# A fused attention and two gated MLPs on one core: MLP blocks of 512 tokens in phases of three ff chunks

## The chip, the cores and the metric

The kernel runs on one core of a Trainium2 chip. The metric is the device time of one execution in microseconds (us). An execution's record gives the span from its first to its last instruction, which is a little shorter than the device time.

## What is computed

Attention with a cumulative bias over 4 batches, 8 heads, 576 positions and head size 64 gives 2304 tokens of 512 features. Two MLPs follow, each with 1536 inner features (ff). The first gates by a sigmoid, the second multiplies two projections:

```python
def _moe_ref(x, w_gate, w_val, w_out):
    gate = 1.0 / (1.0 + np.exp(-(x @ w_gate)))
    val = x @ w_val
    return (gate * val @ w_out).astype(np.float32)

def _moe2_ref(x, w_a, w_b, w_out):
    a = x @ w_a
    b = x @ w_b
    return (a * b @ w_out).astype(np.float32)
```

The activations are float32 and the weights float64 in memory.

## The kernel before

**Attention** goes head by head and ends when all heads' outputs stand, transposed, in `x_sb` (128 partitions x 4 groups of features x 2304 tokens). `attention()` also prepares the first weight tiles on the side. It is emitted in an order by due times and is hardly touched by the change.

**The MLPs** (`mlps`) cut the 1536 inner features of each MLP into 12 chunks of 128, so 24 in all, and take them in phases: six phases of four chunks, three for each MLP. Within a phase all 2304 tokens pass in blocks of `NB` = 384, so a phase has six steps. One step does, for each of its chunks:

- *up* (line 689): one group of matmuls for the gate and one for the value. Every product is made in three passes of 32-bit "round" matmuls (lines 276 to 278), the high half of one operand with the high and the low half of the other, and the low half with the high one. With four groups of features a chunk has 2 x 4 x 3 = 24 matmuls of 128 x `NB`.
- *g* (ACT, line 698) brings the gate out of PSUM, *hf* (DVE, line 702) multiplies it with the value's PSUM bank, *hh* (POOL, line 713) rounds to the high half of h, *hl* (DVE, line 716) subtracts for the low half. h has six tiles, g and hf two each.

Then *dn* (line 727) multiplies the step's h with the output weights. In the first MLP its results stand with features on partitions (four pieces of 128 x `NB`); in the second, with tokens on partitions (one piece of 128 x 512 for each 128 tokens). *ye* adds a piece to what earlier phases left (DVE, line 751), or copies it in the first phase of an MLP (ACT, line 749). The down matmuls of a step must all be issued before the third chunk of the next step goes up (`behind`, line 693). At the start of a step, two halves of the block's input, `xs`, have been made by ACT (line 676) and DVE (line 679).

**Weights** arrive by SP's queue as float64 in three raw buffers of 512 KB each. ACT takes an absolute value (line 224), DVE does four integer and scaling steps (lines 225 to 232), ACT writes the high half (line 243), POOL the low half (line 244). The converted tiles stand in slots: five for the gate matrices, six for the value matrices, six for the output matrices (`NSL`); a tile goes to slot (chunk modulo slots) and is not loaded before the slot's last reader is done. Eight tiles (`early`) are converted wholly within attention; three more have all but their last two steps (lines 243 and 244) done there.

**The order** on each engine is fixed when the program is built. `Schedule.emit` plays the operations through with assumed durations and, on each engine, takes the ready one with the smallest due time. The engines then run in that order and wait by semaphores.

Of the kernel before, what the change touches and what calls it, by code (L numbers as in the profile page):

```python
# [119 lines left out]
def attn_mlp_kernel(  # L120
# [26 lines left out]
    SR = S // NR  # L147
    KD = DM // 128
    KF = DFF // 128
    NB = 384  # L150


    phases = [[0, 1, 2, 3], [4, 5, 6, 7], [8, 9, 10, 11], [12, 13, 14, 15], [16, 17, 18, 19], [20, 21, 22, 23]]
    scale = 1.0 / float(D) ** 0.5
    NEG = -1e9

# [13 lines left out]
    xs0 = const.tile([128, 2, KD, NB], F32R, name="xs0")  # L170


    NSL = [5, 6, 6]
    wt = {}
    early = [(i, m) for m in range(2) for i in range(3)] + [(3, 0), (3, 1)]

    def w_alloc(pool, which):
        for i, m in which:
# [14 lines left out]
    NRAW = 3  # L193
# [428 lines left out]
    def mlps():  # L622
        def tile1(shape, dtype, name):
            return alone(ctx, shape, dtype, name)

        NMX = NB
        h_t = [tile1([128, 2, NMX], F32R, f"h{i}") for i in range(6)]
        g_t = [tile1([128, NMX], FP32, f"g{i}") for i in range(2)]
        hf_t = [tile1([128, NMX], FP32, f"hf{i}") for i in range(2)]
        xs_t = [xs0, tile1([128, 2, KD, NMX], F32R, "xs1")]  # L630
# [12 lines left out]
            "u": [0],  # L643
        })
        op = sc.op
        NP1 = 3

        steps, first, last = [], [], []
        for p in range(len(phases)):
            n = NB  # L650
            first.append(len(steps))
            ts = list(range(0, NT, n))
            steps += [(p, t, n) for t in ts]
            last.append(len(steps) - 1)
        begin = [sum(0.055 * n for _, _, n in steps[:i]) for i in range(len(steps))]
        chain = [None]

        def step(i):
            p, t1, N = steps[i]
            ts = slice(t1, t1 + N)  # L660
            t0 = begin[i]
            MM = 0.00042 * N + 0.001
            cs = phases[p]


# [19 lines left out]
            for e, c in enumerate(cs):  # L685
                for m in range(2):
                    key = (i, c, m)

                    def mm(key=key, c=c, m=m):
                        xs = sc.get("xs", i)  # L690
                        run(passes(sc.get("ps", key)[:, 0:N], wk(c, m), [(xs[:, 0, k, 0:N], xs[:, 1, k, 0:N]) for k in range(KD)]))

                    behind = [("dn", i - 1, d) for d in range(KD)] if e == 2 else []
                    op(("up",) + key, "PE", 12 * MM, mm, xdeps + behind + [("wr", c, m), chain[0]], t0 + 4 * e + 2 * m,
                       acq=("ps", key), rel=("xs", i) if e == len(cs) - 1 and m == 1 else None)
                    chain[0] = ("up",) + key
                g, u = (i, c, 0), (i, c, 1)
                op(("g", i, c), "ACT", 0.06 + N * 0.00083, lambda c=c, g=g: nc.scalar.activation(  # L698
                    out=sc.get("g", (i, c))[:, 0:N], in_=sc.get("ps", g)[:, 0:N],
                    func=ACTF.Sigmoid if p < NP1 else ACTF.Copy), [("up",) + g], t0 + 4 * e + 1,  # L700
                    acq=("g", (i, c)), rel=("ps", g))
                op(("hf", i, c), "DVE", 0.07 + N * 0.00104, lambda c=c, u=u: nc.vector.tensor_tensor(  # L702
                    out=sc.get("hf", (i, c))[:, 0:N], in0=sc.get("ps", u)[:, 0:N], in1=sc.get("g", (i, c))[:, 0:N],
                    op=ALU.mult),
                    [("up",) + u, ("g", i, c)], t0 + 4 * e + 3, acq=("hf", (i, c)), rel=(("ps", u), ("g", (i, c))))
            for e, c in enumerate(phases[p]):
                t = t0 + 4 * e + 3

                def src(c=c):
                    return sc.get("hf", (i, c))[:, 0:N]  # L710

                before = [("hl", i - 1, c2) for c2 in phases[steps[i - 1][0]]] if i else []
                op(("hh", i, c), "Pool", 0.245 + N * 0.00083, lambda c=c, src=src: nc.gpsimd.tensor_scalar(  # L713
                    sc.get("h", (i, c))[:, 0, 0:N], src(), 1.0, 1.0, ALU.mult, ALU.mult),
                    [("hf", i, c)] + before, t, acq=("h", (i, c)))
                op(("hl", i, c), "DVE", 0.07 + N * 0.00104, lambda c=c, src=src: nc.vector.tensor_tensor(  # L716
                    out=sc.get("h", (i, c))[:, 1, 0:N], in0=src(), in1=f32(sc.get("h", (i, c))[:, 0, 0:N]), op=ALU.subtract),
                    [("hh", i, c)], t, rel=("hf", (i, c)))
# [5 lines left out]
            for d in range(pieces):  # L724
                key = (i, "d", d)

                def mm(d=d, key=key):
                    hs = [sc.get("h", (i, c)) for c in phases[p]]
                    ws = [wtile(c, 2) for c in phases[p]]
                    ps = sc.get("ps", key)  # L730
                    sl = slice(d * 128, (d + 1) * 128)
                    if p < NP1:
                        run(passes(ps[:, 0:N], [(w[:, 0, sl], w[:, 1, sl]) for w in ws], [(h[:, 0, 0:N], h[:, 1, 0:N]) for h in hs]))
                    else:
                        run(passes(ps, [(h[:, 0, sl], h[:, 1, sl]) for h in hs], [(w[:, 0], w[:, 1]) for w in ws]))

                n = N if p < NP1 else DM
                op(("dn", i, d), "PE", 3 * len(phases[p]) * MM * n / N, mm, hdeps + wdeps, t0 + 18 + d, acq=("ps", key),
                   rel=tuple(("h", (i, c)) for c in phases[p]) if d == pieces - 1 else None)
                if p < NP1:  # L740
                    dst = y_of[d][:, ts]
                else:
                    dst = acc_sb[:, t1 // 128 + d]
                start = p in (0, NP1)

                def evac(d=d, key=key, dst=dst, n=n, start=start):
                    ps = sc.get("ps", key)[:, 0:n]
                    if start:
                        nc.scalar.copy(out=dst, in_=ps)
                    else:  # L750
                        nc.vector.tensor_tensor(out=dst, in0=ps, in1=dst, op=ALU.add)

                deps = [("dn", i, d)]
                if p == NP1:
                    deps += [("xl", j2, 0) for j2 in range(first[NP1 - 1], first[NP1])]
                op(("ye", i, d), "ACT" if start else "DVE", 0.07 + n * (0.00083 if start else 0.00104), evac, deps,
                   t0 + 18.5 + d, rel=("ps", key))
                if p == len(phases) - 1:
                    r = t1 // 128 + d
                    op(("od", r), "SP", 0.5, lambda r=r, dst=dst: nc.sync.dma_start(  # L760
                        out=out[r * 128:(r + 1) * 128, :], in_=dst), [("ye", i, d)], t0 + 19 + d)

        for i in range(len(steps)):
            step(i)
# [1 line left out]
        for n, m in order:  # L766
# [3 lines left out]
            if o in phase_of:  # L770
                i = last[phase_of[o]]
                deps = [("dn", i, d) for d in range(KD)] if m == 2 else [("up", i, o, m)]
            weights(sc, n, m, deps, begin[first[phase_of[n]]] - 24 + 4 * (n % 4) + (16 if m == 2 else 0), part=1 if (n, m) in order[len(early):len(early) + NRAW] else None)
        sc.emit()

    with tc.manual_schedule():
# [47 lines left out]
```

## Time and profile before

| | |
|---|---|
| time, median of 3 (lowest to highest) | 1149.31 us (1147.91 to 1152.03) |
| profiled execution: its own time, its span | 1150.44 us, 1148.7 us |
| PE busy | 1107.2 us, 6152 matmuls |
| PE weight loads busy | 1039.6 us |
| DVE, ACT, POOL busy | 631.2, 357.7, 299.9 us |
| mean granted TensorE clock | 0.998 |

The busy share of an engine counts its overlapped instructions once. A matmul's own duration in the trace includes its run through the array, which the next matmul overlaps; what a stream of matmuls costs is read from the distance of their starts. A wait printed behind an instruction is the idle time of its engine just before it and the instruction that ended it.

### The profile page before, as it was taken

Reading aid. Unit: us, or ns where it says so; the run is one execution under the profiler, and the core shown is the slowest. Engines: PE = TensorE matmul, PEld = TensorE weight load, DVE = VectorE, ACT = ScalarE, POOL = GpSimd, SP = SyncE. Lnnn points to the kernel's source line nnn. Section 1 sums busy time; section 2 is a strip of 40 time slices with the busy share of each in tenths; the row PEclk is TensorE's granted clock in tenths of the full one; section 3 lists DMA queues with packets and bytes.
Section 4 is the critical chain, followed back from the end, with each engine's and each line's share of the span. In section 5 each row is a group of like instructions: output and inputs, shape, how many; then the busy total and the mean of one; then the engine's idle time right before and its main releaser. Section 6 shows DMA issues by size and latency. Waiting matters only on the chain.

```text
span 1148.7 us, 16112 instructions
## 1 busy us (share of the span) xinstructions
PE 1107.2 (96%) x6152; PEld 1039.6 (91%) x6152; DVE 631.2 (55%) x1015; ACT 357.7 (31%) x635; POOL 299.9 (26%) x364
## 2 busy tenths in 40 slices
PE   2999999999999999999999999999999999999998
PEld 1787777798999999999999999899999999999997
DVE  5788788728223783337943369522487334653322
ACT  2575666534122431112311133322343111322100
POOL 2245555554001340002410024200233101311100
PEclk9999999999999999999999999999999999999999
DMA  3566676533000230002310013200122000200001
GB/s 110 149 180 159 172 171 161 135 92 111 1 1 18 79 109 16 1 1 74 102 46 1 1 43 105 74 1 1 37 92 92 1 1 3 71 28 29 29 28 55
DMA packets 69743, 74.08 MB, mean 64 GB/s; under 512 B 28551, under 2 KB 53311, under 8 KB 69666
## 3 DMA queue, kind: packets, MB, share of 16 engines
q1 hardware_dynamic: 66514, 68.08, 20.7%
q10 hardware_dynamic: 2896, 4.81, 1.7%
q8 instruction: 49, 0.80, 0.3%
q14 instruction: 28, 0.23, 0.1%
q0 software_dynamic: 256, 0.15, 0.1%
HBM read 57.65 MB, written 5.60 MB: 55 GB/s over the span
## 4 chain that ended last, share of the span: by engine, by line
PE 78%; DVE 8%; DMA 5%; POOL 3%; issue 3%; ACT 2%; SPq 0%; ACTq 0%; POOLq 0%; DVEq 0%
PE ps L277 22%; PE ps L278 22%; PE ps L276 22%; PE ps_x L570 5%; PE ps_g L498 2%; DVE u L227 2%; POOL w L244 1%; DVE raw L229 1%; DVE h L716 1%; DVE hf L702 1%; DVE raw L232 1%; PE ps_e L535 1%; PE ps_e L536 1%; DVE u L225 1%; PE ps_g L503 1%
## 5 line engine op out<-in xcount | busy, mean ns | idle before, releaser
L276 PE MATMUL ps<-xs,w 128*128 128x384 f32 x1152 | 385.0, 334 | 0.0
L278 PE MATMUL ps<-xs,w 128*128 128x384 f32 x1152 | 385.0, 334 | 0.0
L277 PE MATMUL ps<-xs,w 128*128 128x384 f32 x1152 | 384.9, 334 | 0.0
L713 POOL TENSOR_SCALAR h<-hf 128x384 fp32r<-128x384 f32 x144 | 91.9, 638 | 576.8 <-DVE hf L702 576.8
L702 DVE TENSOR_TENSOR hf<-ps,g 128x384 f32<-128x384 f32 x144 | 79.9, 555 | 281.7 <-PE ps L278 280.9
L276 PEld LDWEIGHTS ps<-xs,w 128*128 128x128 f32 x1152 | 216.3, 188 | 0.7
L277 PEld LDWEIGHTS ps<-xs,w 128*128 128x128 f32 x1152 | 216.3, 188 | 0.7
L278 PEld LDWEIGHTS ps<-xs,w 128*128 128x128 f32 x1152 | 216.3, 188 | 0.0
L698 ACT ACTIVATE g<-ps 128x384 f32<-128x384 f32 x144 | 70.8, 491 | 435.4 <-PE ps L278 435.3
L244 POOL TENSOR_TENSOR w<-raw,w 128x512 fp32r<-128x512 f32 x72 | 101.0, 1403 | 131.9 <-ACT w L243 129.2
L716 DVE TENSOR_TENSOR h<-hf,h 128x384 fp32r<-128x384 f32 x144 | 88.9, 618 | 83.1 <-POOL h L713 83.1
L276 PE MATMUL ps<-h,w 128*128 128x384 f32 x288 | 97.3, 338 | 2.2 <-POOL h L713 2.0
L278 PE MATMUL ps<-h,w 128*128 128x384 f32 x288 | 97.0, 337 | 2.1 <-POOL w L244 2.1
L570 PE MATMUL ps_x<-pt,vx 128*128 128x320 f32 (+4 forms) x448 | 95.6, 365 | 2.3 <-DMA vx<-in_vm_dram 1.1
L277 PE MATMUL ps<-h,w 128*128 128x384 f32 x288 | 97.0, 337 | 0.6 <-DVE h L716 0.6
L511 DVE TENSOR_REDUCE nm<-ps_g 128x1 f32<-128x512 f32 (+4 forms) x160 | 77.0, 531 | 37.1 <-PE ps_g L503 37.0
L570 PEld LDWEIGHTS ps_x<-pt,vx 128*128 128x128 f32 x448 | 76.1, 191 | 19.8 <-ACT xt L579 1.6
L277 PE MATMUL ps<-w,h 128*128 128x512 f32 x216 | 84.6, 392 | 1.0 <-POOL w L244 0.9
L278 PE MATMUL ps<-w,h 128*128 128x512 f32 x216 | 84.4, 391 | 0.0
L276 PE MATMUL ps<-w,h 128*128 128x512 f32 x216 | 84.1, 389 | 0.0
L557 POOL TENSOR_SCALAR_AFFINE_SELECT pt<-pt 128x256 f32<-128x256 f32 (+1 forms) x96 | 51.5, 558 | 114.4 <-ACT pt L541 113.7
L243 ACT CAST w<-raw 128x512 fp32r<-128x512 f32 x72 | 47.2, 659 | 104.6 <-DVE raw L232 103.0
(92 smaller groups left out, 1328.3 us busy)
## 6 DMA issues: line engine op xcount, KB each, us to landing
raw<-in_moe_w_out_dram SPq DMA_DIRECT2D x24, 512.0 KB
r<-in_qk_dram SPq DMA_DIRECT2D x32, 288.0 KB
raw<-in_moe_w_gate_dram SPq DMA_DIRECT2D x12, 512.0 KB
raw<-in_moe_w_val_dram SPq DMA_DIRECT2D x12, 512.0 KB
raw<-in_moe_w_a_dram SPq DMA_DIRECT2D x12, 512.0 KB
raw<-in_moe_w_b_dram SPq DMA_DIRECT2D x12, 512.0 KB
o<-o ACTq DMA_DIRECT2D x32, 144.0 KB
o<-o SPq DMA_DIRECT2D x32, 144.0 KB
```

Of the source, the lines that this page charges most:

```text
L243: ("ACT", 0.53, lambda: nc.scalar.copy(out=wtile(n, m)[:, 0], in_=value())),
L244: ("Pool", 1.23, lambda: nc.gpsimd.tensor_tensor(out=wtile(n, m)[:, 1], in0=value(), in1=f32(wtile(n, m)[:, 0]), op=ALU.subtract)),
L276: nc.tensor.matmul(out=outp, lhsT=wh, rhs=xh, start=(e == 0), stop=False)
L277: nc.tensor.matmul(out=outp, lhsT=wh, rhs=xl, start=False, stop=False)
L278: nc.tensor.matmul(out=outp, lhsT=wl, rhs=xh, start=False, stop=(e == n - 1))
L511: nc.vector.tensor_reduce(out=nm[0:n, c:c + 1], in_=ps[0:n, p0:p0 + nk], axis=AX.X, op=ALU.max)
L557: nc.gpsimd.affine_select(to, to, [[0, 2], [1, n]][2 - w:], ALU.is_ge, 0.0, base=0, channel_multiplier=-1)
L570: nc.tensor.matmul(out=px[:, 256 + a:256 + q1_], lhsT=vx[:, j], rhs=pt[:, p0:p0 + q1_ - a], start=j == 0, stop=j == js[-1])
L698: op(("g", i, c), "ACT", 0.06 + N * 0.00083, lambda c=c, g=g: nc.scalar.activation(out=sc.get("g", (i, c))[:, 0:N], in_=sc.get("ps", g)[:, ...
L702: op(("hf", i, c), "DVE", 0.07 + N * 0.00104, lambda c=c, u=u: nc.vector.tensor_tensor(out=sc.get("hf", (i, c))[:, 0:N], in0=sc.get("ps", ...
L713: op(("hh", i, c), "Pool", 0.245 + N * 0.00083, lambda c=c, src=src: nc.gpsimd.tensor_scalar(sc.get("h", (i, c))[:, 0, 0:N], src(), 1.0, 1 ...
L716: op(("hl", i, c), "DVE", 0.07 + N * 0.00104, lambda c=c, src=src: nc.vector.tensor_tensor(out=sc.get("h", (i, c))[:, 1, 0:N], in0=src(), ...
```

## The change

Blocks have 512 tokens: four full ones and one of 256 in each phase. A phase has three chunks, so there are eight phases of five steps in place of six phases of six. The slots become 5, 5 and 4, the early tiles six, the tiles of h four. The planner's assumed duration of a matmul, its due times and the place of `behind` (now the second chunk of a step) follow.

```diff
-    NB = 384
+    NB = 512
-    phases = [[0, 1, 2, 3], [4, 5, 6, 7], [8, 9, 10, 11], [12, 13, 14, 15], [16, 17, 18, 19], [20, 21, 22, 23]]
+    phases = [[3 * i, 3 * i + 1, 3 * i + 2] for i in range(2 * KF // 3)]
...
-    NSL = [5, 6, 6]
+    NSL = [5, 5, 4]
     wt = {}
-    early = [(i, m) for m in range(2) for i in range(3)] + [(3, 0), (3, 1)]
+    early = [(i, m) for m in range(2) for i in range(3)]
...
-        h_t = [tile1([128, 2, NMX], F32R, f"h{i}") for i in range(6)]
+        h_t = [tile1([128, 2, NMX], F32R, f"h{i}") for i in range(4)]
...
-        NP1 = 3
+        NP1 = len(phases) // 2
...
-            n = NB
             first.append(len(steps))
-            ts = list(range(0, NT, n))
-            steps += [(p, t, n) for t in ts]
+            steps += [(p, t, min(NB, NT - t)) for t in range(0, NT, NB)]
             last.append(len(steps) - 1)
-        begin = [sum(0.055 * n for _, _, n in steps[:i]) for i in range(len(steps))]
+        begin = [sum(0.048 * n for _, _, n in steps[:i]) for i in range(len(steps))]
...
-            MM = 0.00042 * N + 0.001
+            MM = 0.00042 * N + 0.013
+            f = N / 384
...
-                    behind = [("dn", i - 1, d) for d in range(KD)] if e == 2 else []
-                    op(("up",) + key, "PE", 12 * MM, mm, xdeps + behind + [("wr", c, m), chain[0]], t0 + 4 * e + 2 * m,
+                    behind = [("dn", i - 1, d) for d in range(KD)] if e == 1 else []
+                    op(("up",) + key, "PE", 12 * MM, mm, xdeps + behind + [("wr", c, m), chain[0]], t0 + f * (4 * e + 2 * m),
...
-            weights(sc, n, m, deps, begin[first[phase_of[n]]] - 24 + 4 * (n % 4) + (16 if m == 2 else 0), part=1 if (n, m) in order[len(early):len(early) + NRAW] else None)
+            weights(sc, n, m, deps, begin[first[phase_of[n]]] - 24 + 5 * (n % 3) + (16 if m == 2 else 0), part=1 if (n, m) in order[len(early):len(early) + NRAW] else None)
```

The due times of the other operations of a step are scaled by `f` in the same way. The built program has 720 PE rows fewer (5274 in place of 5994). Three pieces of the order are shown, since the prediction speaks of them. Lines below the first edit that removes a line stand one lower in the changed kernel (L701 there is L702 here). Names are the tiles with their numbers: `h2` is a tile of h, `hf` the product before it is split, `u` and `mag` scratch tiles of the weight conversion, `raw` a weight tile as it arrived, `w3_0` the slot 3 of the gate matrices.

**DVE, first step of the first MLP.** Before, from the second *hf* to the third:

```order
L702 TENSOR_TENSOR hf1_2389<-ps3_2449,g1_2381 128x384
L225 TENSOR_SCALAR u_73<-raw_2498 128x512
L227 SCALAR_TENSOR_TENSOR u_73<-raw_2498,u_73 128x512
L716 TENSOR_TENSOR h1_2357<-hf1_2389,h1_2357 128x384
L229 SCALAR_TENSOR_TENSOR raw_2498<-raw_2498,u_73 128x512
L232 SCALAR_TENSOR_TENSOR raw_2498<-mag_74,raw_2498 128x512
L702 TENSOR_TENSOR hf0_2385<-ps5_2457,g0_2377 128x384
```

Now, from behind the first *hl* to the third *hf*:

```order
L225 TENSOR_SCALAR u_71<-raw_2466 128x512
L227 SCALAR_TENSOR_TENSOR u_71<-raw_2466,u_71 128x512
L229 SCALAR_TENSOR_TENSOR raw_2466<-raw_2466,u_71 128x512
L232 SCALAR_TENSOR_TENSOR raw_2466<-mag_72,raw_2466 128x512
L701 TENSOR_TENSOR hf1_2361<-ps3_2417,g1_2353 128x512
L225 TENSOR_SCALAR u_71<-raw_2469 128x512
L227 SCALAR_TENSOR_TENSOR u_71<-raw_2469,u_71 128x512
L715 TENSOR_TENSOR h1_2337<-hf1_2361,h1_2337 128x512
L229 SCALAR_TENSOR_TENSOR raw_2469<-raw_2469,u_71 128x512
L232 SCALAR_TENSOR_TENSOR raw_2469<-mag_72,raw_2469 128x512
L225 TENSOR_SCALAR u_71<-raw_2484 128x512
L701 TENSOR_TENSOR hf0_2357<-ps5_2425,g0_2349 128x512
```

The second *hf* now stands behind the four steps of a weight tile, and the third behind those of a second tile and the first step of a third; before, one tile's steps lay ahead of the third.

**POOL, the same place.** Before:

```order
L244 TENSOR_TENSOR w2_2_2405<-raw_2076,w2_2_2405 128x512
L713 TENSOR_SCALAR h0_2353<-hf0_2385 128x384
L713 TENSOR_SCALAR h1_2357<-hf1_2389 128x384
L244 TENSOR_TENSOR w3_2_2409<-raw_2498,w3_2_2409 128x512
L713 TENSOR_SCALAR h2_2361<-hf0_2385 128x384
L713 TENSOR_SCALAR h3_2365<-hf1_2389 128x384
```

Now:

```order
L244 TENSOR_TENSOR w2_2_2377<-raw_1695,w2_2_2377 128x512
L712 TENSOR_SCALAR h0_2333<-hf0_2357 128x512
L712 TENSOR_SCALAR h1_2337<-hf1_2361 128x512
L244 TENSOR_TENSOR w3_0_2385<-raw_2466,w3_0_2385 128x512
L244 TENSOR_TENSOR w3_1_2389<-raw_2469,w3_1_2389 128x512
L712 TENSOR_SCALAR h2_2341<-hf0_2357 128x512
L712 TENSOR_SCALAR h3_2345<-hf1_2361 128x512
```

One low half of a weight tile (w3_2) stood between the second and the third *hh*; now two stand there (w3_0 and w3_1).

**DVE, the end of the first phase.** Before, from a step of 384 tokens to the next (the last one) and the first weight tile of the next phase:

```order
L702 TENSOR_TENSOR hf1_2389<-ps7_2465,g1_2381 128x384
L716 TENSOR_TENSOR h1_2357<-hf1_2389,h1_2357 128x384
L679 TENSOR_TENSOR xs0_64<-x_sb_61,xs0_64 128x1536
L702 TENSOR_TENSOR hf0_2385<-ps1_2441,g0_2377 128x384
L716 TENSOR_TENSOR h2_2361<-hf0_2385,h2_2361 128x384
L225 TENSOR_SCALAR u_73<-raw_3331 128x512
L227 SCALAR_TENSOR_TENSOR u_73<-raw_3331,u_73 128x512
```

Now, from the last step of 512 tokens to the step of 256 and the first weight tile:

```order
L701 TENSOR_TENSOR hf1_2361<-ps3_2417,g1_2353 128x512
L715 TENSOR_TENSOR h3_2345<-hf1_2361,h3_2345 128x512
L678 TENSOR_TENSOR xs1_2365<-x_sb_61,xs1_2365 128x2048
L701 TENSOR_TENSOR hf0_2357<-ps5_2425,g0_2349 128x256
L715 TENSOR_TENSOR h0_2333<-hf0_2357,h0_2333 128x256
L225 TENSOR_SCALAR u_71<-raw_2973 128x512
L227 SCALAR_TENSOR_TENSOR u_71<-raw_2973,u_71 128x512
```

The *hl* that ends a full block is followed by the input split of the next phase's first block and then by the first *hf* of the 256-token step; no weight step stands between the last *hf* and *hl* of the full block here. In later phases weight steps stand on both sides of this place.

## Rows read from the trace of the kernel before

**Rows 1.** The page: span, PE's busy time, chain that ended last by engine.
```profile
span 1148.7 us, 16112 instructions
...
PE 1107.2 (96%) x6152; PEld 1039.6 (91%) x6152; DVE 631.2 (55%) x1015; ACT 357.7 (31%) x635; POOL 299.9 (26%) x364
...
PE 78%; DVE 8%; DMA 5%; POOL 3%; issue 3%; ACT 2%; SPq 0%; ACTq 0%; POOLq 0%; DVEq 0%
```

**Rows 2.** Busy us of each engine by stretch, instructions, clock, DMA share, GB/s.
```profile
258.00:272.00 14.00, 11.40 (x53) 10.13 (x52) 12.92 (x17) 6.54 (x12) 6.37 (x6) 0.88 0.24 77
272.00:380.00 108.00, 108.00 (x625) 108.00 (x625) 39.22 (x58) 28.80 (x49) 16.03 (x23) 1.00 0.10 30
```

**Rows 3.** Timeline of PE, up, 384 wide: start us, us, instruction (24 starts apart).
```profile
1079.82 0.33 PE L276 MATMUL ps<-xs,w 128*128 128x384 f32 x1
...
1083.98 0.33 PE L276 MATMUL ps<-xs,w 128*128 128x384 f32 x1
```

**Rows 4.** Timeline of PE, down in the second MLP, 512 wide (0, 10, 13 and 35 starts in).
```profile
1136.32 0.39 PE L276 MATMUL ps<-w,h 128*128 128x512 f32 x1
...
1138.62 0.39 PE L277 MATMUL ps<-w,h 128*128 128x512 f32 x1
...
1139.31 0.39 PE L277 MATMUL ps<-w,h 128*128 128x512 f32 x1
...
1144.29 0.39 PE L278 MATMUL ps<-w,h 128*128 128x512 f32 x1
```

**Rows 5.** Timeline of PE in attention: one 320-wide matmul, then two 192 wide.
```profile
206.53 0.31 PE L536 MATMUL ps_f<-o 128*128 128x320 f32 x1
206.68 0.25 PE L535 MATMUL ps_f<-o 128*128 128x192 f32 x1
...
206.88 0.19 PE L535 MATMUL ps_t<-o 128*64 128x64 f32 x1
```

**Rows 6.** Timeline of PE, first matmul of the MLPs and their first down stage.
```profile
237.45 0.42 PE L276 MATMUL ps<-xs,w 128*128 128x384 f32 x1
...
259.21 0.34 PE L278 MATMUL ps<-h,w 128*128 128x384 f32 x1
...
263.21 0.63 PE L276 MATMUL ps<-h,w 128*128 128x384 f32 x1 [1.04 <-POOL h L713]
...
266.80 0.34 PE L277 MATMUL ps<-h,w 128*128 128x384 f32 x1
```

**Rows 7.** Timelines of POOL, ACT and DVE in the first step of the MLPs.
```profile
249.06 3.83 POOL L244 TENSOR_TENSOR w<-raw,w 128x512 fp32r<-128x512 f32 x3
...
258.25 1.31 POOL L244 TENSOR_TENSOR w<-raw,w 128x512 fp32r<-128x512 f32 x1 [3.11 <-ACT w L243]
...
254.08 0.69 ACT L224 ACTIVATE mag<-raw 128x512 f32<-128x512 f32 x1 [9.55 <-DMA raw<-in_moe_w_out_dram]
...
257.40 0.55 DVE L702 TENSOR_TENSOR hf<-ps,g 128x384 f32<-128x384 f32 x1
...
258.31 1.80 DVE L227 SCALAR_TENSOR_TENSOR u<-raw,u 128x512 int32<-128x512 int32 x1
```

**Rows 8.** PE at the start of the second phase (timeline, 4 starts apart); PE's waits.
```profile
418.81 0.34 PE L278 MATMUL ps<-h,w 128*128 128x384 f32 x1
...
421.21 0.34 PE L276 MATMUL ps<-h,w 128*128 128x384 f32 x1
...
PE ps L278 <- POOL w L244: 2.1, 2, 1.3
```

**Rows 9.** Groups by form: busy us, mean ns of one, idle before and releaser.
```profile
L713 POOL TENSOR_SCALAR h<-hf 128x384 fp32r<-128x384 f32 x144 | 91.9, 638 | 576.8 <-DVE hf L702 576.8
L716 DVE TENSOR_TENSOR h<-hf,h 128x384 fp32r<-128x384 f32 x144 | 88.9, 618 | 83.1 <-POOL h L713 83.1
L751 DVE TENSOR_TENSOR x_sb<-ps,x_sb 128x512 f32<-128x512 f32 x36 | 24.8, 689 | 46.0 <-PE ps L278 46.0
```

**Rows 10.** Timeline of PE: the last wait within attention.
```profile
234.61 0.48 PE L570 MATMUL ps_x<-pt,vx 128*128 128x256 f32 x1 [0.98 <-ACT xt L579]
```

More of the change, by code (lines that the diff above doesn't have):

```diff
@@ L699, in step @@
                     out=sc.get("g", (i, c))[:, 0:N], in_=sc.get("ps", g)[:, 0:N],
-                    func=ACTF.Sigmoid if p < NP1 else ACTF.Copy), [("up",) + g], t0 + 4 * e + 1,
+                    func=ACTF.Sigmoid if p < NP1 else ACTF.Copy), [("up",) + g], t0 + f * (4 * e + 1),
                     acq=("g", (i, c)), rel=("ps", g))
@@ L704, in step @@
                     op=ALU.mult),
-                    [("up",) + u, ("g", i, c)], t0 + 4 * e + 3, acq=("hf", (i, c)), rel=(("ps", u), ("g", (i, c))))
+                    [("up",) + u, ("g", i, c)], t0 + f * (4 * e + 3), acq=("hf", (i, c)), rel=(("ps", u), ("g", (i, c))))
             for e, c in enumerate(phases[p]):
-                t = t0 + 4 * e + 3
+                t = t0 + f * (4 * e + 3)
                 def src(c=c):
@@ L737, in step @@
                 n = N if p < NP1 else DM
-                op(("dn", i, d), "PE", 3 * len(phases[p]) * MM * n / N, mm, hdeps + wdeps, t0 + 18 + d, acq=("ps", key),
+                op(("dn", i, d), "PE", 3 * len(phases[p]) * MM * n / N, mm, hdeps + wdeps, t0 + f * 13 + d, acq=("ps", key),
                    rel=tuple(("h", (i, c)) for c in phases[p]) if d == pieces - 1 else None)
@@ L756, in step @@
                 op(("ye", i, d), "ACT" if start else "DVE", 0.07 + n * (0.00083 if start else 0.00104), evac, deps,
-                   t0 + 18.5 + d, rel=("ps", key))
+                   t0 + f * 13 + 0.5 + d, rel=("ps", key))
                 if p == len(phases) - 1:
@@ L760, in step @@
                     op(("od", r), "SP", 0.5, lambda r=r, dst=dst: nc.sync.dma_start(
-                        out=out[r * 128:(r + 1) * 128, :], in_=dst), [("ye", i, d)], t0 + 19 + d)
+                        out=out[r * 128:(r + 1) * 128, :], in_=dst), [("ye", i, d)], t0 + f * 13 + 1 + d)
         for i in range(len(steps)):
```

## The prediction

> **What bounds the kernel now.** The page comes first: PE is busy for 96% of the span and holds 78% of the chain that ended last [rows 1]; DVE, the next, is busy for 55%. By stretches, the MLPs are one unbroken stream of matmuls, as from 272 to 380 us, where PE is busy for all of the 108 us at the full clock, while DVE works for a third of it [rows 2]. So two things can change the time: what the stream costs per matmul, and the places where it breaks.
>
> The stream is priced by the distance of starts. At 384 columns 24 starts take 4.16 us, 173.3 ns each [rows 3]. At 512 columns, in the down stage of the second MLP, a quiet stretch of 22 starts takes 4.98 us, 226.4 ns each; the 10 starts ahead of it, beside the last step's *hf*, *hh* and *hl*, take 2.30 us, 230 ns each; all 35 average 227.7 [rows 4]. A line through 173.3 at 384 and 227.0 at 512 has 0.42 ns per column and 12.2 ns that each matmul costs whatever its width.
>
> The breaks: from the first MLP matmul to the start of the last one 906.8 us pass [rows 6, 4]. Of 384 columns there are 24 chunks x 24 x 6 blocks = 3456 up and 12 x 12 x 6 = 864 down matmuls, together 4320; of 512 columns 18 x 12 x 3 = 648. They stream in 4320 x 0.1733 + 648 x 0.2277 = 896.2 us; with the last one's 0.2 us added to the stretch, 10.8 us are lost. 5.2 of them lie in the first down stage: 4 starts take 4.00 us, 3.3 more than they need, and the 10 behind them 3.59 us, 1.9 more [rows 6]; the granted clock of this stretch is 0.88 [rows 2], so after the wait the matmuls run partly at 1.2 GHz. The other 5.6 are mostly the five later starts of a phase, about one each: at the first, 4 starts take 2.40 us where 0.69 would do, 1.7 lost, and PE waits for the low half of an output weight tile on POOL [rows 8].
>
> **Part 1, wider matmuls.** The columns stay the same, 2304 per chunk. Up and down of the first MLP go from 4320 matmuls of 384 to 2880 of 512 and 720 of 256; the 648 of the second MLP's down stage stay. Before 4320 x 173.3 = 748.7 us. Now 2880 x 227.0 = 653.8, and by the line 256 columns cost 119.6, so 720 x 119.6 = 86.1; together 739.9. **Gain 8.8 us**, which is 720 fewer matmuls at 12.2 ns. All of it lies on PE, hence on the path. Bounds: 226.4 ns at 512 makes it 10.1, 227.7 makes it 7.3, and 230 throughout only 2.3. I take 227.0, nearer the quiet rows, because the 384-wide up stage keeps its 173 ns in a long stretch with DVE and POOL at work (108 us for 625 matmuls, [rows 2]). The 256-wide form is not in the trace for this kind of operand; a 320-wide matmul takes 0.15 us to the next start and two 192-wide ones 0.20 [rows 5], so 256 lies between 0.10 and 0.15. Its middle, 0.125, would take 3.9 us of the gain away.
>
> The Trainium skill, "TensorE: Matmul & The Clock Gate", section "Wait — 56ns, not 53.3ns?", gives a matmul's fixed cost at full clock as about 2.5 ns; by that 720 fewer would save only an estimated 1.8 us. The trace disagrees at 384 columns, where the start distance lies 13.3 ns above 384/2.4 GHz, and I keep the rows' price.
>
> **Part 2, the first down stage.** Here the order gets worse. Before, the low halves of three output tiles end on POOL at 252.9 and the first weight load of the MLPs has landed at 254.1 [rows 7]; neither depends on the block, so I keep both. Now the second *hf* stands behind four DVE steps of that tile: before, these and an *hl* took until 257.4 [rows 7], so it starts near 257.0 and, at 0.69 us for 512 columns out of PSUM [rows 9], ends at 257.7. *hh* takes 0.64 at 384 [rows 9], so some 0.7 now: 258.4. POOL then holds w3_0 for 1.3 us [rows 7], to 259.8. DVE instructions beside this POOL operation stretch to 1.80 us [rows 7], so the second *hl* ends near 260.3; two steps of the second tile and one of the third (0.6 to 0.7 each by the 257.4 row) bring the third *hf* to 262.8. POOL's w3_1 needs the second tile's last step and ACT's cast, so it runs from 262.4 to 263.8, and the third *hh* ends at 264.5. Its *hl* comes at about 265.9, behind two more steps. PE gets there earlier: 96 up matmuls and 6 down at 0.227 from 237.45 [rows 6] make 260.6. It waits 3.8 us, then 1.3 more, then has some 9 matmuls at the low clock, 1.9 as before: 7.0 in place of 5.2, **1.8 us lost**. Bounds: 0, if the pieces overlap more, and 4, if the gate tile (now the first to be loaded) lands 2 us after the output tile that led before.
>
> **Part 3, the starts of phases.** There are seven in place of five. Each is lighter: chunks whose slot frees only in the phase's last step were 3 gate, 2 value and 2 output tiles, and are now 1, 1 and 2. The two late output tiles decide. They wait for the old phase's last down matmuls; from there to the new phase's first down stage PE had two chunks up, two more of the next block, and three chunks down, 48 x 0.1733 x 2 + 9 x 0.1733 = 18.2 us, and has now 72 x 0.227 + 6 x 0.227 = 17.7. DVE's own work there is a third longer per instruction. I take 0.7 us for each, 4.9 in all against the 5.6: **gain 0.7**. Bounds: all vanish, a gain of 5.6; each costs the 1.7 of [rows 8], a loss of 6.3.
>
> **Part 4, the seam.** A full block's last *hf*, *hh* and *hl* (0.69 + 0.7 + 0.8, [rows 9] scaled to 512) take 2.2 us and three handovers. Mostly a chunk of 24 x 0.227 = 5.4 us and the first two chunks' down matmuls, 1.4, cover them. Ahead of the 256-token block the chunk lasts 24 x 0.12 = 2.9 us, so the cover is 4.3. In the first phase no weight step is in the way; later ones have them. I take **0.3 us lost** over eight, bounds 0 and 8.
>
> **Part 5, attention.** Two weight tiles fewer are converted there. PE's last wait in it, 0.98 us for ACT, is all I see that could shrink [rows 10]: gain 0 to 1.0, **0.4** taken. The larger input splits and the more frequent sums (*ye* of six accumulating phases, not four) fall to DVE and ACT, which have room [rows 2]; they cost nothing while DVE is that idle. The end, one *ye* and one store after the last matmul, stays.
>
> **Sum.** -8.8 + 1.8 - 0.7 + 0.3 - 0.4 = -7.8 us. The profiled execution took 1150.44, so 1142.6 for such a one; it lies 1.1 above the median of 1149.31, so the forecast is **1141.5**.
>
> **The rivals.**
> *The saving is spent on waits.* The first down stage costs 4 and the phase starts 1.2 each (8.4 against 5.6): -8.8 + 4 + 2.8 = -2, so 1147.3. For it: the orders shown pile weight steps ahead of *hf* and *hh*. Against: fewer late tiles per start.
> *A wide matmul saves almost nothing.* At 230 ns all the way the gain is 2.3, and the sum -1.3: 1148.0. By the Trainium skill's fixed cost ("TensorE: Matmul & The Clock Gate", the same section) it would be near that too, an estimated 1148.5. For it: the disturbed starts of [rows 4]. Against: the quiet ones, and the 13.3 ns at 384.
> *The seams break the stream.* If weight steps hold DVE and POOL at each of the eight seams, as the 1.80 us row shows one can, the 2.2 us chain grows to 6 or more against a cover of 4.3. From 1.0 us each the gain is gone (-7.8 + 8); at 2 us each the time is 1149.3 - 7.8 + 16 = 1157.5, slower than before. Against: in the first phase the order leaves the place free.
> *The stops vanish.* With four late tiles in place of seven each start of a phase is free, and the first stage costs no more than before: -8.8 - 5.6 + 0.3 - 0.4 = -14.5, so 1134.8.
>
> **How the numbers follow.** Forecast 0.70, spent on waits 0.11, nothing saved by width 0.04 (0.02 of it by the page's price), seams 0.05, stops vanish 0.10. A measurement of this kernel can tell about 0.3%, 3.4 us, from no change: faster is below 1145.9. Of the forecast's own spread 0.04 lies beyond that line, and of the seams 0.01 stays within it: faster 0.66 + 0.10 = 0.76, same 0.04 + 0.11 + 0.04 + 0.01 = 0.20, slower 0.04. The range leaves out the seams and part of the vanishing stops: 1136 to 1147.8.
>
> **What would show it.** Starts of 512-wide up matmuls 226 to 228 ns apart and of 256-wide ones near 120 confirm part 1; 230 and more refute it. The first down stage should lose about 7 us behind POOL's third *hh*, with a dip of the clock. Each start of a phase should lose under 1.5 us on POOL's low half, each seam under 0.5 on *hl*. The forecast is wrong if the stream breaks elsewhere, above all on an input split (`xs`) or a late up tile.

## The result, and the profile after

The changed kernel takes 1138.80 us, the median of 6 runs (1135.02 to 1139.34). The kernel before, on the same chip, takes 1150.01 us, the median of 6 (1147.91 to 1153.42). The ratio is 0.9891, with an interval of 0.987 to 0.9912. The forecast was 1141.5 us, with a range of 1136.0 to 1147.8. The direction and the range were right; the gain, 11.2 us by these medians, was 3.4 larger than the 7.8 of the forecast.

The profiled execution of the changed kernel took 1139.34 us, 11.1 less than that of before. Three lines of its page, which answer to [rows 1]:

```profile
span 1137.5 us, 14567 instructions
...
PE 1094.5 (96%) x5432; PEld 916.2 (81%) x5432; DVE 674.3 (59%) x1005; ACT 370.5 (33%) x615; POOL 302.6 (27%) x340
...
PE 83%; DVE 8%; DMA 3%; issue 2%; ACT 1%; POOL 1%; SPq 0%; ACTq 0%; DVEq 0%; POOLq 0%
```

PE has 720 matmuls fewer (5432 in place of 6152) and a larger share of the chain: 83% in place of 78%. DVE is busier by 43 us, and its share of the chain stays at 8%. PE's busy share did not move (96%), so it can't tell the gain.

The stretches, as in [rows 2] (busy us of PE, PEld, DVE, ACT and POOL, each with its instructions; clock, DMA share, GB/s):

```profile
256.00:270.00 14.00, 9.42 (x33) 6.79 (x32) 13.79 (x16) 6.37 (x10) 6.72 (x6) 0.88 0.25 77
270.00:376.00 106.00, 106.00 (x520) 89.95 (x519) 53.76 (x68) 37.35 (x57) 22.13 (x24) 1.00 0.15 45
```

The picture of before is kept: one stretch with a hole and a granted clock of 0.88, then an unbroken stream at the full clock. The stream of after has 520 matmuls in 106 us, that of before had 625 in 108.

The price of a matmul is read, as in [rows 3, 4], from the distance of starts on PE's timeline (start us, us, instruction). Up at 512 columns, 24 starts apart; then the last 256-wide starts of a step and the first 512-wide one behind them:

```profile
294.66 0.39 PE L276 MATMUL ps<-xs,w 128*128 128x512 f32 x1
...
300.10 0.39 PE L276 MATMUL ps<-xs,w 128*128 128x512 f32 x1
...
348.11 0.28 PE L276 MATMUL ps<-xs,w 128*128 128x256 f32 x1
...
349.55 0.40 PE L276 MATMUL ps<-xs,w 128*128 128x512 f32 x1
```

5.44 us for 24 is 226.7 ns each, 13.3 above 512/2.4 GHz; 1.44 us for 12 is 120.0 ns each, 13.3 above 256/2.4 GHz. The 173.3 of [rows 3] lies 13.3 above 384/2.4 GHz. So an up matmul costs 13.3 ns beside its columns, at all three widths. The durations in the rows (0.39 and 0.28 us) don't show this.

The first down stage, which answers to [rows 6] (PE, POOL and DVE, apart):

```profile
259.38 0.40 PE L278 MATMUL ps<-h,w 128*128 128x512 f32 x1
263.46 0.50 PE L276 MATMUL ps<-h,w 128*128 128x512 f32 x1 [3.69 <-POOL h L712]
264.60 0.79 PE L277 MATMUL ps<-h,w 128*128 128x512 f32 x1 [0.64 <-DVE h L715]
265.19 0.63 PE L278 MATMUL ps<-h,w 128*128 128x512 f32 x1
265.62 0.63 PE L276 MATMUL ps<-h,w 128*128 128x512 f32 x1
```
```profile
256.71 1.73 POOL L244 TENSOR_TENSOR w<-raw,w 128x512 fp32r<-128x512 f32 x1
261.09 1.30 POOL L244 TENSOR_TENSOR w<-raw,w 128x512 fp32r<-128x512 f32 x1 [2.65 <-ACT w L243]
262.35 1.06 POOL L712 TENSOR_SCALAR h<-hf 128x512 fp32r<-128x512 f32 x1
```
```profile
257.19 1.79 DVE L715 TENSOR_TENSOR h<-hf,h 128x512 fp32r<-128x512 f32 x1
...
260.57 0.68 DVE L701 TENSOR_TENSOR hf<-ps,g 128x512 f32<-128x512 f32 x1
261.17 1.76 DVE L227 SCALAR_TENSOR_TENSOR u<-raw,u 128x512 int32<-128x512 int32 x1
```

Two low halves of weight tiles (L244) stand on POOL between the second and the third *hh* (L712). The third *hf* ended near 261.2, but its *hh* could start only at 262.35, behind the second of them. PE waits 3.69 us, then 0.64 for the *hl*, and its next starts are 0.43 us apart where 0.227 would do: the low level, 1.2 GHz.

**The whole account.** For each kernel below, the distances of starts from the first MLP matmul to the last were split in two: the *stream* is the number of matmuls of each width times the mean distance of those starts that lie within 30 ns of the usual one; the rest is *lost* (waits, and matmuls at the low clock).

| | matmuls from there on | stream us | lost us | first MLP matmul us |
|---|---|---|---|---|
| before | 4968 | 896.7 | 10.1 | 237.45 |
| after | 4248 | 886.5 | 10.7 | 235.82 |

Stream -10.2, losses +0.6, start of the MLPs -1.6: together -11.2, which is the difference of the spans (1148.7 and 1137.5). All but 0.1 us of the losses lies in the first down stage of a phase, in both kernels.

### The profile page after: what moved, and what is told of

Its sections match the earlier page's. It is cut to its first block, busy times and chain, and to the rows that moved or that the text cites. A ratio compares the mean times of both kernels' runs of the same rounds, so it can differ in the third digit from the quotient of the medians.

```text
span 1137.5 us, 14567 instructions
## 1 busy us (share of the span) xinstructions
PE 1094.5 (96%) x5432; PEld 916.2 (81%) x5432; DVE 674.3 (59%) x1005; ACT 370.5 (33%) x615; POOL 302.6 (27%) x340
## 4 chain that ended last, share of the span: by engine, by line
PE 83%; DVE 8%; DMA 3%; issue 2%; ACT 1%; POOL 1%; SPq 0%; ACTq 0%; DVEq 0%; POOLq 0%
PE ps L278 24%; PE ps L277 24%; PE ps L276 23%; PE ps_x L570 6%; PE ps_g L498 2%; DVE raw L229 2%; DVE u L227 1%; PE ps_e L536 1%; PE ps_e L535 1%; PE ps_g L503 1%; DMA relq_d<-ya_sb 1%; DVE raw L232 1%; DVE nm L511 1%; DMA o<-relq_d 1%; POOL w L244 1%
## 5 line engine op out<-in xcount | busy, mean ns | idle before, releaser
L276 PE MATMUL ps<-xs,w 128*128 128x512 f32 (+1 forms) x960 | 353.3, 368 | 0.0
L277 PE MATMUL ps<-xs,w 128*128 128x512 f32 (+1 forms) x960 | 353.2, 368 | 0.0
L278 PE MATMUL ps<-xs,w 128*128 128x512 f32 (+1 forms) x960 | 353.1, 368 | 0.0
L712 POOL TENSOR_SCALAR h<-hf 128x512 fp32r<-128x512 f32 (+1 forms) x120 | 89.9, 749 | 527.4 <-DVE hf L701 527.4
L701 DVE TENSOR_TENSOR hf<-ps,g 128x512 f32<-128x512 f32 (+1 forms) x120 | 76.3, 635 | 254.5 <-PE ps L278 247.9
L277 PEld LDWEIGHTS ps<-xs,w 128*128 128x128 f32 x960 | 181.0, 189 | 30.2
L276 PEld LDWEIGHTS ps<-xs,w 128*128 128x128 f32 x960 | 181.0, 189 | 30.2
L278 PEld LDWEIGHTS ps<-xs,w 128*128 128x128 f32 x960 | 181.0, 189 | 29.9
L697 ACT ACTIVATE g<-ps 128x512 f32<-128x512 f32 (+1 forms) x120 | 66.5, 554 | 392.2 <-PE ps L278 391.9
L244 POOL TENSOR_TENSOR w<-raw,w 128x512 fp32r<-128x512 f32 x72 | 105.0, 1460 | 170.0 <-ACT w L243 164.8
L715 DVE TENSOR_TENSOR h<-hf,h 128x512 fp32r<-128x512 f32 (+1 forms) x120 | 82.8, 690 | 70.1 <-POOL h L712 70.1
L276 PE MATMUL ps<-h,w 128*128 128x512 f32 (+1 forms) x240 | 88.9, 370 | 3.7 <-POOL h L712 3.7
L277 PE MATMUL ps<-h,w 128*128 128x512 f32 (+1 forms) x240 | 89.5, 373 | 1.2 <-DVE h L715 1.2
L278 PE MATMUL ps<-h,w 128*128 128x512 f32 (+1 forms) x240 | 89.2, 372 | 1.4 <-POOL w L244 1.4
```

What stands on the lines that cost most here:

```text
L244: ("Pool", 1.23, lambda: nc.gpsimd.tensor_tensor(out=wtile(n, m)[:, 1], in0=value(), in1=f32(wtile(n, m)[:, 0]), op=ALU.subtract)),
L276: nc.tensor.matmul(out=outp, lhsT=wh, rhs=xh, start=(e == 0), stop=False)
L277: nc.tensor.matmul(out=outp, lhsT=wh, rhs=xl, start=False, stop=False)
L278: nc.tensor.matmul(out=outp, lhsT=wl, rhs=xh, start=False, stop=(e == n - 1))
```

## The experiments

Times are medians; ratios stand against runs of the kernel before on the same chip taken in the same sitting. Its own median lay between 1147.55 and 1150.3 us in the three sittings, so where times of different sittings are close, the ratios and the account decide.

### The first down stage: the next phase's tiles loaded later

```diff
             deps = [("dn", i, d) for d in range(KD)] if m == 2 else [("up", i, o, m)]
+            if not deps and phase_of[n] == 1:
+                deps = [("hl", 0, phases[0][-1])]
```

> The changed kernel, with the weight tiles of the second phase ordered behind the first step's last hl. Theory A (the 6.8 us lost in the first down stage come from weight steps that stand ahead of hf and hh on DVE and POOL): the first hh still waits for POOL until about 251, then hf, hh and hl of three chunks follow without weight steps and end near 257, before PE arrives at 257.6; 5.5 to 6.8 us less than the changed kernel, about 1132. Theory B (POOL's tail of attention and the three low halves of output tiles are what PE waits for, the weight steps only fill their shadow): less than 2 us gained, 1137 or more.

Measured: 1130.38 us (1129.81 to 1134.03), ratio 0.9837 [0.9815, 0.9859], against 0.9891 for the changed kernel. The losses fall from 10.7 to 3.6 us, the stream stays (886.5). POOL and DVE now go through the place like this:

```profile
250.90 0.62 POOL L712 TENSOR_SCALAR h<-hf 128x512 fp32r<-128x512 f32 x1 [1.41 <-DVE hf L701]
252.93 0.62 POOL L712 TENSOR_SCALAR h<-hf 128x512 fp32r<-128x512 f32 x1 [1.41 <-DVE hf L701]
260.99 1.31 POOL L244 TENSOR_TENSOR w<-raw,w 128x512 fp32r<-128x512 f32 x1 [7.44 <-ACT w L243]
```
```profile
251.55 0.69 DVE L715 TENSOR_TENSOR h<-hf,h 128x512 fp32r<-128x512 f32 x1 [0.74 <-POOL h L712]
252.16 0.68 DVE L701 TENSOR_TENSOR hf<-ps,g 128x512 f32<-128x512 f32 x1
253.58 0.69 DVE L715 TENSOR_TENSOR h<-hf,h 128x512 fp32r<-128x512 f32 x1 [0.74 <-POOL h L712]
```

No weight step stands between *hf*, *hh* and *hl*, the *hl* takes 0.69 in place of 1.79 us, and the first down stage loses 0.2 us in place of 7.0. So its cause is shown: tiles that only the second phase needs were converted in front of the first phase's h.

> The kernel before, with one edit: the tiles of the second phase may be loaded only after the first step's last hl. Nothing of the computation changes. If the first down stage waits in both kernels because steps of the next phase's tiles stand between hf and hh (theory A), the loss there falls from 5.2 us to 0 to 1 and the time by about 5: 1144 to 1146 us. If it is the three late output tiles of the first phase itself (theory B), which this edit leaves in place, the loss stays near 5 and the time near 1150. The first MLP matmul should come as in the kernel before, near 237.5 us, if the 1.6 us that the changed kernel gained there belong to the two early tiles; near 235.5 if they are a scatter between runs.

This is the same edit in the kernel before. Measured: 1145.42 us against 1147.55 for the kernel before, ratio 0.9982 [0.9968, 0.9996]; losses 6.6 in place of 10.1 us. The first down stage loses 2.2 in place of 5.2, between the two theories: the greater part was the next phase's tiles. What is left is the first phase's own fourth output tile, which is still converted there (POOL's timeline):

```profile
254.67 1.33 POOL L244 TENSOR_TENSOR w<-raw,w 128x512 fp32r<-128x512 f32 x1 [3.12 <-ACT w L243]
255.95 0.53 POOL L713 TENSOR_SCALAR h<-hf 128x384 fp32r<-128x384 f32 x1
257.63 0.51 POOL L713 TENSOR_SCALAR h<-hf 128x384 fp32r<-128x384 f32 x1 [1.14 <-DVE hf L702]
```

With phases of three chunks that tile does not exist: the first phase needs nine, and six early tiles and three half-prepared ones are nine. So the change made a free first stage possible, and its order used the place for other tiles.

### Six early tiles in the kernel before

```diff
-    early = [(i, m) for m in range(2) for i in range(3)] + [(3, 0), (3, 1)]
+    early = [(i, m) for m in range(2) for i in range(3)]
```

> The kernel before with six early tiles in place of eight, as in the changed kernel; all else as before. If the two tiles cost attention time (theory A), the first MLP matmul comes 1 to 2 us earlier than 237.45, near 235.8; the two tiles of the fourth chunk are then converted in the first step of the MLPs and may cost a wait there, so the time lies between 1147 and 1152. If they cost nothing (theory B), the first MLP matmul stays at 237.5 and the time is 1149 to 1153.

Measured: 1150.52 us, ratio 1.0023 [1.001, 1.0036]; losses 14.1 us, 4.0 more than before, all of it in the first down stage (PE's timeline):

```profile
260.31 0.45 PE L278 MATMUL ps<-h,w 128*128 128x384 f32 x1 [0.28 <-POOL w L244]
266.46 0.69 PE L276 MATMUL ps<-h,w 128*128 128x384 f32 x1 [5.71 <-ACT w L243]
```

Six early tiles alone are no gain: with four chunks in the first phase the missing ones are waited for. The first MLP matmul came at 233.27 us, far earlier than either theory had it, which put the question of attention to more executions.

> The kernel before, unchanged, profiled once more for the time of its first MLP matmul. If the 1.6 us by which attention ended earlier in the changed kernel belong to the two early tiles (theory A), it lies again near 237.5 us, above all eight kernels with six early tiles (232.8 to 235.9). If it is a scatter between executions (theory B), it lies anywhere from 233 to 237.5, as in the kernel before with late weights, where it was 234.1 with eight tiles.

> The same once more, the kernel before unchanged, so that four executions with eight early tiles stand against eight with six. Theory A: near 237.5 us again. Theory B: from 233 to 237.5, a mean within 1 us of that of the kernels with six tiles, 234.6.

Measured: 1151.33 and 1147.43 us, first MLP matmul at 237.86 and 233.29. The same kernel, unchanged, so moves by 4.6 us here. All executions together: with eight early tiles 237.45, 237.86, 234.09 and 233.29, a mean of 235.7; with six 232.81 to 236.07 over ten kernels, a mean of 234.9. Theory B holds: 1.6 us between two executions tells nothing, and what the two tiles cost in attention, 0.8 by these means, is not told from the scatter. The difference of the medians, 11.2 us, is touched less, since both are medians of six.

### The starts of phases: a fifth output slot

```diff
-    NSL = [5, 5, 4]
+    NSL = [5, 5, 5]
```

This goes on top of the late weights.

> As the kernel with the second phase's weight tiles behind the first step, and with a fifth slot for the output tiles, so that one output tile in place of two waits for its slot at the start of a phase. Theory A (the four starts of a phase that lose 0.6 to 1.0 us each lose it on the second late output tile): 3 to 4 us less than that kernel, about 1128 to 1129. Theory B (they lose it on something else, an hl or a DVE step beside POOL): the same within 1 us.

Measured: 1129.5 us (1125.45 to 1130.83), ratio 0.9817 [0.9793, 0.9841]. Losses 1.1 us, of which 0.6 at one start of a phase, 0.4 in the first down stage and none at the other starts. In the changed kernel four of seven starts lost 0.6, 1.0, 1.0 and 1.0 us. The three of 1.0 waited for the low half of an output tile, like this one:

```profile
488.83 0.39 PE L277 MATMUL ps<-h,w 128*128 128x512 f32 x1
489.95 0.50 PE L278 MATMUL ps<-h,w 128*128 128x512 f32 x1 [0.73 <-POOL w L244]
```

The first of them, at the start of the second phase, waited for a *hl* (PE's and DVE's timelines of the changed kernel):

```profile
377.76 0.50 PE L277 MATMUL ps<-h,w 128*128 128x512 f32 x1 [0.33 <-DVE h L715]
```
```profile
375.91 1.79 DVE L715 TENSOR_TENSOR h<-hf,h 128x512 fp32r<-128x512 f32 x1 [0.52 <-POOL h L712]
```

With five slots only one output tile of a phase waits for the old phase's last down matmuls, and that one comes in time: the three waits are gone. The wait for *hl* stays; it is the 0.6 that is left. So theory A held for three of the four starts, theory B for one. The gain in the MLPs is 2.5 us (losses 3.6 to 1.1), a little under what theory A expected for four; the medians alone (1130.38 and 1129.5) would not tell it from nothing, the traces do.

### What the width is worth: more matmuls, the same columns

Back to 384 tokens in the changed kernel:

```diff
-    NB = 512
+    NB = 384
```

> Phases of three, 14 slots and four tiles of h, but blocks of 384 as before. Theory A (the gain is the fixed cost of each matmul, 13.3 ns, and nothing else of the change matters): up and down matmuls are 4320 again, so +9.6 us on the changed kernel, about 1148 to 1149. Theory B (the wider block also carries the smaller number of slots: with 384 columns the time between the release of a slot and its next reader shrinks from 17.7 us to 24 x 3 x 0.1733 + 6 x 0.1733 = 13.5 us, while the two late output tiles need as long as before): each of the seven starts of a phase loses some 3 to 6 us, 20 to 40 us in all, about 1165 to 1190. The trace tells them apart by the starts of the phases.

Measured: 1200.91 us, ratio 1.0437 [1.0415, 1.0459]. The stream is 897.3, 10.8 longer than in the changed kernel, near theory A's price. But the losses are 62.8 us, far more than even theory B expected: 52.5 in the first down stages of the seven later phases and 9.0 in that of the first. PE's waits (line waited for, releaser: us in total, times, longest), and the second phase's first down stage:

```profile
PE ps L276 <- ACT w L243: 19.4, 7, 4.0
PE ps L277 <- POOL w L244: 6.5, 6, 1.6
PE ps L278 <- POOL w L244: 5.4, 5, 1.6
```
```profile
376.80 0.41 PE L276 MATMUL ps<-h,w 128*128 128x384 f32 x1 [1.95 <-ACT w L243]
377.05 0.34 PE L277 MATMUL ps<-h,w 128*128 128x384 f32 x1
378.77 0.69 PE L278 MATMUL ps<-h,w 128*128 128x384 f32 x1 [1.39 <-POOL w L244]
379.25 0.52 PE L276 MATMUL ps<-h,w 128*128 128x384 f32 x1
...
384.06 0.52 PE L276 MATMUL ps<-h,w 128*128 128x384 f32 x1
```

The late output tiles of the seven starts cost 31.3 us of waits, 4.5 each; in the changed kernel three of them cost 0.7 to 0.8. The prediction's own sum gives the size: PE's time from the old phase's last down matmuls to the new phase's first ones is 78 matmuls, 17.7 us at 227 ns and 13.5 at 173.3, so 4.2 us of cover are gone. 16 us more are 103 starts that lie 30 to 250 ns late, nearly all at the low clock behind the waits: the 15 distances of starts from 379.25 to 384.06 are 0.32 us each. So with 5, 5 and 4 slots, phases of three chunks stand only with wide blocks; the two halves of the change belong together. Wide blocks with phases of four chunks were not run.

To have the width without late tiles, 384 tokens and six slots for each matrix, on the late weights:

```diff
-    NB = 512
+    NB = 384
...
-    NSL = [5, 5, 5]
+    NSL = [6, 6, 6]
```

> The version with late weights and five output slots, with blocks of 384 tokens and six slots for each matrix, so that no tile of a next phase is late. Nothing of the computation changes. It is meant to leave the width alone between the two. If a matmul costs 13.3 ns beside N/2.4 GHz (theory A), 720 more matmuls cost 9.6 us: 1129.5 + 9.6 = 1139, with the starts of phases free of waits. If 384-wide phases of three chunks break for another reason than late tiles (theory B: the conversion of nine tiles does not fit a phase of 384-token steps), the starts lose several us each as with 384 and 5, 5, 4 slots, and the time is 1155 to 1200.

Measured: 1152.48 us against 1147.55 for the kernel before, ratio 1.0033 [1.0018, 1.0049]. The stream is 897.3, against 886.5 of the version with 512 tokens: theory A's price again. The losses are 15.6 us, so the time is nearer to theory B. No start of a phase waits for a weight tile any more. But 11.1 us are still lost in the first down stages of phases two to seven, and 3.1 in the first two steps of the first phase, where PE waits for h. DVE's timeline in the second step of the first phase, then in the first step of the fourth:

```profile
268.20 1.78 DVE L229 SCALAR_TENSOR_TENSOR raw<-raw,u 128x512 int32<-128x512 int32 x1
269.91 2.06 DVE L678 TENSOR_TENSOR xs<-x_sb,xs 128x1536 fp32r<-128x1536 f32 x1
271.89 0.55 DVE L715 TENSOR_TENSOR h<-hf,h 128x384 fp32r<-128x384 f32 x1
...
592.16 0.68 DVE L232 SCALAR_TENSOR_TENSOR raw<-mag,raw 128x512 f32<-128x512 f32 x1
592.76 2.06 DVE L678 TENSOR_TENSOR xs<-x_sb,xs 128x1536 fp32r<-128x1536 f32 x1
594.74 1.64 DVE L715 TENSOR_TENSOR h<-hf,h 128x384 fp32r<-128x384 f32 x1
```

The last *hl* of the step stands behind a weight step and an input split, and PE's down matmuls wait for it (5.4 us over the seven waits of line 277, 1.6 over three of line 278). That is the third rival's mechanism, and here it shows with blocks of 384.

Then two cuts of the 2304 tokens that leave first and last blocks alone, on the late weights and five slots; one row of the diff for each:

```diff
-            steps += [(p, t, min(NB, NT - t)) for t in range(0, NT, NB)]
+            steps += [(p, t, n) for t, n in ((0, 512), (512, 256), (768, 256), (1024, 512), (1536, 512), (2048, 256))]
```
```diff
+            steps += [(p, t, n) for t, n in ((0, 512), (512, 384), (896, 384), (1280, 384), (1664, 384), (2048, 256))]
```

> The version with late weights and five output slots, with blocks of 512, 256, 256, 512, 512 and 256 tokens: one block of 512 is cut into two of 256. The columns stay; 576 more up and 144 more down matmuls, 720, as many as the change took away. If a matmul costs 13.3 ns beside N/2.4 GHz at every width (theory A), the stream is 9.6 us longer: 1129.5 + 9.6 = 1139.1, plus what the shorter steps of 256 tokens may wait, 0 to 4 us, which the trace shows apart. If the fixed cost of a matmul is 2.5 ns or is hidden (theory B), the stream grows by 1.8 us or less, and the time is 1131 where nothing waits.

> The version with late weights and five output slots, with blocks of 512, 384, 384, 384, 384 and 256 tokens: three blocks of 512 are cut into four of 384. Again 720 more matmuls with the same columns. Theory A (13.3 ns each at every width): 1139.1 us and no long waits, since no step is as short as one of 256 tokens but the last. Theory B (2.5 ns or less): 1131. Both runs at 1139 would show that the count of matmuls is what the change saves by, whichever widths they have.

Measured: 1147.91 us, ratio 0.9975 [0.9963, 0.9987], and 1144.56 us, ratio 0.9953 [0.9933, 0.9972]. All versions with the same columns, by the account above:

| blocks of a phase | matmuls | stream us | lost us |
|---|---|---|---|
| before, 6 x 384 | 4968 | 896.7 | 10.1 |
| 6 x 384 in phases of three chunks | 4968 | 897.3 | 15.6 |
| 512, 256, 256, 512, 512, 256 | 4968 | 896.6 | 9.2 |
| 512, 4 x 384, 256 | 4968 | 897.4 | 6.9 |
| after, 4 x 512, 256 | 4248 | 886.5 | 10.7 |
| the same with late weights and five slots | 4248 | 886.5 | 1.1 |

The stream goes by the count of matmuls, whichever widths they have: 720 more cost 10.1 to 10.9 us, 14 to 15 ns each. Of that, 9.6 us are the 13.3 ns; most of the rest goes with the 512-wide down matmuls of the second MLP, whose starts lie 227.4 to 228.4 ns apart in these versions and 227.0 in the changed kernel. Theory A's price holds in all of them, theory B's in none. The times lie above A's 1139 by the losses, which both expectations had too low; the version cut to 384, which was to have no long waits, has three for *hl* of 1.3 to 1.4 us. In both versions the losses lie in the first down stages of phases. In the version cut to 256 they are the waits of the down matmuls ahead of a short step:

```profile
PE ps L277 <- DVE h L715: 4.0, 4, 1.3
PE ps L278 <- DVE h L715: 1.6, 3, 0.8
```
```profile
368.23 1.70 DVE L227 SCALAR_TENSOR_TENSOR u<-raw,u 128x512 int32<-128x512 int32 x1
369.85 1.63 DVE L678 TENSOR_TENSOR xs<-x_sb,xs 128x1024 fp32r<-128x1024 f32 x1
371.40 0.68 DVE L715 TENSOR_TENSOR h<-hf,h 128x512 fp32r<-128x512 f32 x1
```

A chunk of a 256-token step covers 2.9 us and, with the first two chunks' down matmuls, the prediction's 4.3. A weight step and an input split ahead of the *hl* take 3.3, and *hf*, *hh* and *hl* come on top. The same step from 512 to 256 tokens lost nothing at the end of any phase, and nothing in the first down stage of the eighth phase, which comes after DVE's last weight step (1041 us). So the short step alone does not break the stream.

### Blocks of 512 and 384 with the same number of matmuls

```diff
+            steps += [(p, t, n) for t, n in ((0, 512), (512, 512), (1024, 512), (1536, 384), (1920, 384))]
```

> The changed kernel with blocks of 512, 512, 512, 384 and 384 tokens in place of four of 512 and one of 256: as many matmuls and columns as the changed kernel, but no 256-wide ones. Theory A (a matmul costs 13.3 ns besides its columns, at every width): 2160 x 0.2268 + 1440 x 0.1733 = 739.4 us against 739.6, so the same time, within 2 us. Theory B (the 256-wide matmuls or the seam ahead of the short block cost something of their own): 1 to 8 us faster. Where the last block is longer, the phase's late tiles are released at another distance: the starts of phases may move by a microsecond each.

Measured, in the changed kernel: 1145.86 us, ratio 0.9966 [0.9952, 0.9981], 7 us slower than the changed kernel, where no theory had it slower; only the last sentence of the expectation named the place. The stream is 887.7, nearly the same; the losses are 16.5 in place of 10.7 us, and the additional ones lie at the starts of phases, the largest as waits of 2.0 and 1.9 us for the low half of an output tile.

> The version with late weights and five output slots, with blocks of 512, 512, 512, 384 and 384 tokens in place of four of 512 and one of 256. Matmuls and columns are the same in number, so the stream is. If the 7 us that these blocks lost in the changed kernel came from the late output tile at the starts of phases (theory A), they are gone here: 1129.5 +- 1.5 us. If another wait of the 384-token block took them (theory B, input splits or h tiles), 1134 to 1137.

Measured, on the late weights and five slots: 1129.1 us (1128.8 to 1130.41), ratio 0.9837 [0.9817, 0.9857]; stream 887.5, losses 0.7. This version and the one with late weights and five slots (1129.5 us, ratio 0.9817) are the fastest that were run; the two can't be told apart. So the 7 us belonged to the late tiles, not to the blocks of 384 as such. By which step of the tiles' chain a longer last block delays them in the changed kernel was not settled.

## Why the prediction was right, point by point

Each term beside what the two profiles show, in us:

| term | forecast | shown |
|---|---|---|
| wider matmuls | -8.8 | -10.2 |
| first down stage | +1.8 | +1.8 (5.2 to 7.0) |
| starts of phases | -0.7 | -1.3 (4.9 to 3.6) |
| seam | +0.3 | 0 |
| attention | -0.4 | -1.6, scatter |
| sum | -7.8 | -11.2 (of unrounded terms) |

- **Part 1** had the right mechanism, and the stream gained 1.4 more than it had. The line of [rows 3, 4] gave 12.2 ns for each matmul, because 227.0 at 512 columns came from rows partly disturbed; the rows of after give 13.3 (226.7 and 120.0). That is 0.8 of it. 0.6 more is the second MLP's down stage, which the prediction took to stay as it was: its 512-wide starts lay 227.9 ns apart on the mean and now lie 227.0 apart. Without that stage the gain is 9.6, within its bound of 10.1. The 125 ns that it allowed for 256 columns did not come.

By the Trainium skill, "TensorE: Matmul & The Clock Gate", section "Wait — 56ns, not 53.3ns?", with about 2.5 ns of fixed cost, 720 matmuls would be worth an estimated 1.8 us. Five kernels with 720 matmuls more show 10.1 to 10.9. The measurement decides.

- **Part 2** was right to 0.1 us in its sum and right in its order of steps: the wait of 3.8 for POOL's third *hh* was 3.69 in the row (3.86 by the starts), the 1.3 behind it 1.3 (0.91 and 0.36), the low clock 1.3 where 1.9 was forecast; 0.5 for the second *hl* had not been forecast. These last two misses cancel, so the agreement to 0.1 is in part luck. Its *hh* of 0.7 was not the 0.64 of [rows 9] scaled to 512 columns (0.85); rows of after show 0.62 to 1.06. All times lay 1 to 2 us earlier than worked out; the MLPs began 1.6 earlier. That the late weights make it vanish shows the cause.
- **Part 3** had the direction and, for the greater part, the place (the late output tiles), and forecast 0.7 for each of seven. Three lost 1.0 there, one 0.6 on a *hl*, which this part had not, and three nothing: 3.6 in all. The kernel before lost 4.9 at its five starts, not the 5.6 that this part took. The version with 384 tokens fits the sum of the cover: 4.2 us less cover, and waits of 4.5 in place of 0.8 or less.
- **Part 4**: the seam lost nothing, the lower bound. The mechanism is real, since the cuts that put a shorter step behind the first of a phase show it there, with weight steps on DVE. In the changed kernel the short step is the last of a phase, and at that place the cut to 256 loses nothing either.
- **Part 5** can't be judged: 1.6 between two executions lies within the 4.6 by which the kernel before moves by itself. This step failed as a term of a sum over two single executions: the 0.98 us wait of [rows 10] was no measure of what it would take.
- **The rivals.** *The saving is spent on waits*: losses rose by 0.6, not by 6.8. *Nothing saved by width* is refuted by the five streams of 4968 matmuls. *The seams* did not break. *The stops vanish* did not come about by the change itself, but what it would give is now measured: 1129.5 with the two small edits, below the 1134.8 of that rival, mostly because the first down stage goes too (5.2 to 0.4).

## What to carry to other kernels

When a kernel is one unbroken stream of matmuls, count them: here each costs 13 to 15 ns beside its columns, so the wider blocks won by their smaller number, and the distance of starts tells it before anything is changed. Then look at the few holes that are left: at the first use of data, work for a later phase must not stand in the queues of the engines that prepare it, and a buffer's slots should be enough that few of the next phase's tiles wait for the old phase's end (here one of the output tiles was few enough, two were not). Shorter phases need the cover of longer steps, so check the time between last use and first use of a slot in matmuls times their distance.

## What was not expected of the hardware

- The 13.3 ns beside the columns is the same at 256, 384 and 512 columns (120.0, 173.3 and 226.7 ns): the three widths lie 13.3 ns above N/2.4 GHz, N being the columns.
- DVE's *hl* and weight steps took 1.7 to 1.8 us beside POOL's L244 in place of 0.69: the *hl* of 1.79 at 257.19 beside POOL's 1.73 at 256.71, against 0.69 for the same *hl* in the version with late weights, where POOL is idle. The prediction used this for one row; it showed again in L227 at 261.17 and 368.23 and in L229 at 268.20, where POOL's L244 ran from 261.09, 368.05 and 268.12.
- Waits differ in what they cost behind them. After 1.95 and 1.39 us, with two matmuls between them, 15 matmuls ran at the low level, 0.32 us apart (379.25 to 384.06); after a single wait of 0.73 us (489.95) the next start came 0.34 us later and the ones behind it at the full rate (0.23).
- Attention's end moves by 4.6 us between executions of one kernel, more than most of the terms of this sum.
